# Attention scores of two heads in the two row halves of TensorE, and a first tile cut by batch

## Chip, cores and metric

One core of a Trainium2 chip. The metric is the device time of one execution in microseconds (us), lower is better.

## What is computed

A sliding-window attention (window 128, linear bias by head), then a mixture of four experts, then one dense layer with a squared ReLU, all in float32:

```python
# q, k, v: 2 batches, 8 heads, 576 positions, 64 per head
scores = q @ k.transpose(0, 1, 3, 2) / sqrt(64)
mask = (rel >= 0) & (rel < 128)                 # rel = query - key position
scores = where(mask, scores - slope[head] * abs(rel), -1e9)
attn = exp(scores - max(scores)); attn = attn / (sum(attn) + 1e-9)
x = (attn @ v), heads side by side              # 1152 tokens x 512
p = probs / (sum(probs) + 1e-9)
x = sum over e of p[:, e] * (relu(x @ w1[e]) @ w2[e])     # 4 experts, 512 -> 1024 -> 512
out = relu(x @ w_in) ** 2 @ w_out                          # 512 -> 2048 -> 512
```

## The kernel before

**Precision.** Matrices that need float32 results are split: `hi` is the value rounded to fp32r, `lo` the rest, and a product is hi·hi + lo·hi + hi·lo in fp32r, three passes of TensorE. Some early products go in plain fp32 instead, so that nothing has to be split first; each such matmul stands as two records in the profile.

**Stages.** The program has one long first stage, in which attention, the first expert's first product (g1, `hps`) and its second product (g2, `yacc`) for the first three chunks of tokens are interleaved, and then the remaining chunk, experts 1 to 3 and the dense layer. The first stage's order is made by a planner, class `Plan` (line 38): every piece of work is a task with engines that could run it and a modelled time on each, tasks it depends on, buffers it takes and a due time. `run` picks, again and again, the engine that can start first and of its tasks the most urgent one, and records that task's instructions. Each engine then executes its instructions in that order. What follows the first stage is written by another scheduler and is not touched by the change.

**Attention units.** `units` (line 627) lists the work: 4 units for query tile 0 (128 positions), each with two heads of both batches (four score matrices), then 8 units for tiles 1 and 2 and 8 for tiles 3 and 4, each two heads of one batch. Tile 4 has 64 positions and is called twin. For one unit and tile, `job_tasks` (line 833) makes the chain: scores on TensorE (`sc`, line 856), join of the two key tiles (`copy_predicated`, DVE), bias and row minimum (L917, DVE), exp (L926, ACT), inverse of the sum (DVE), scaling (POOL, ACT or DVE), transposes on TensorE (`tp`, L966), copy out (`pt`), mask halves (POOL). `pv` (line 757) then multiplies with v, two heads side by side in the two column halves of the array (`xps`: L764 in tile 0, L778 later).

**Scores.** For tiles 1 to 4, q comes twice from memory, in partitions 0 to 63 and again in 64 to 127, and k is split so that its hi part is in partitions 0 to 63 and its lo part in 64 to 127 of one tile (`khl`). So one matmul over all 128 rows gives qh·kh + qh·kl, a second one ql·kh + ql·kl: two matmuls a head, four a pair of heads (L879; twins L863). Tile 0 is not split: plain fp32 of 64 rows, always in the array's first 64 rows (L871):

```python
for g in range(G):
    if raw:
        nc.tensor.matmul(out=sc[0:n, g, :], lhsT=first_in["q", c // 2][0:D, ...],
                         rhs=first_in["k", c // 2][0:D, ...], start=True, stop=True)
        continue
    for ql in (b_["qh"].tile, b_["ql"].tile):
        nc.tensor.matmul(out=sc[0:n, g, :], lhsT=ql[:, qs], rhs=b_["khl"].tile[:, g, j0:j0 + w], ...)
```

**First tokens.** q, k and v of tile 0 are loaded by `first_load` and `first_v` (lines 1656 and 1667), then the first weights. As soon as tile 0's attention output (`xfirst`) is there, g1 starts with plain fp32 for the first four column blocks (L1839, both batches in one matmul of 256 columns), and its g2 is L1790. Later g1 is L1051 and g2 is L1287. Until there is real work, and in gaps that the planner foresees, `keep_busy` (line 554) fills TensorE with small bfloat16 matmuls on a zero tile (L560).

Of the kernel before, what the change touches and what calls it, by code (L numbers as in the profile page):

```python
# [16 lines left out]
P = 128  # L17
# [12 lines left out]
class Buf:  # L30
# [3 lines left out]
    def __init__(self, kind):  # L34
        self.kind, self.users, self.end, self.tile = kind, 0, 0.0, None


class Plan:
# [7 lines left out]
    COLD = 3.0  # L46
    WARM = 24.0
    HELD = 0.65
    SLOWED = 0.3

    def __init__(self, slots):
        self.tasks = []
        self.slots = slots
        self.held = {k: [] for k in slots}
        self.at = dict(PE=0.0, ACT=0.0, DVE=0.0, POOL=0.0, SP=0.0)
        self.port = dict(POOL=None, DVE=None)

    def add(
        self, name, opts, fn, deps=(), takes=(), bufs=(), due=0.0, follow=(), cold=True,
        shared=False  # L60
    ):
        t = dict(
            name=name, opts=opts, fn=fn, deps=[d for d in deps if d], takes=list(takes),
            bufs=list(takes) + list(bufs), due=due, end=None, follow=[d for d in follow if d],
            cold=cold, shared=shared,
        )
        for b in t["bufs"]:
            b.users += 1
        self.tasks.append(t)
        return t  # L70

    def ready(self, t):
        r = 0.0
        for d in t["deps"]:
            if d["end"] is None:
                return None
            r = max(r, d["end"] + 0.08)
        for d in t["follow"]:
            if d["end"] is None:
                return None  # L80
            r = max(r, d["start"])
        want = {}
        for b in t["takes"]:
# [3 lines left out]
            if i >= 0:  # L87
                if held[i].users:
# [4 lines left out]
    def run(self, until=None):  # L93
        todo = self.tasks
        while todo and not (until and until()):
            cand = []
            for t in todo:
# [4 lines left out]
                for eng, occ, lat in t["opts"]:  # L102
                    start = max(self.at[eng], r)
# [4 lines left out]
                cand.append((best, t))  # L108
            assert cand, [t["name"] for t in todo[:20]]
            first, _ = min(cand, key=lambda c: c[0][1])  # L110
            eng, start = first[0], first[1]
            (eng, start, occ, lat), t = min(
                (c for c in cand if c[0][0] == eng and c[0][1] <= start + self.LOOK),
                key=lambda c: c[1]["due"],
            )
            other = self.port["POOL" if eng == "DVE" else "DVE"]
            if other and (eng == "POOL" or eng == "DVE" and t["shared"]):
# [3 lines left out]
                else:  # L121
# [4 lines left out]
                    self.at["POOL"] = max(self.at["POOL"], other["start"] + other["occ"])  # L126
                occ, lat = occ + more, lat + more
            t["start"], t["end"], t["occ"] = start, start + lat, occ
            self.gap = start - self.at[eng] if start < self.WARM else 0.0
            self.at[eng] = start + occ  # L130
            if eng == "POOL" or eng == "DVE" and t["shared"]:
                self.port[eng] = t
            for b in t["takes"]:
                self.held[b.kind].append(b)
            t["fn"](eng)
            for b in t["bufs"]:
                b.users -= 1
                b.end = max(b.end, t["end"])
            todo.remove(t)
# [3 lines left out]
def kernel(  # L143
# [346 lines left out]
    def last_runs(nt):  # L490
# [17 lines left out]
        rq=3, rk=2, rv=4, qh=2, ql=2, khl=2, sc=2, tp=2, ts=5, st=5, pt=4, work=2, y=2, h=4  # L508
# [6 lines left out]
        sc=[actx.enter_context(tc.tile_pool(name="psc", bufs=2, space=PSUM))],  # L515
# [111 lines left out]
    units = [dict(bs=(0, 1), t0=0, t1=1, c=c, col=0) for c in range(NP)]  # L627
# [8 lines left out]
    task = {}  # L636

# [5 lines left out]
    def unit_tasks(u, due):  # L643
        d = units[u]
        bs, t0, t1, c = d["bs"], d["t0"], d["t1"], d["c"]
        nb = len(bs)
        G = 2 * nb
# [3 lines left out]
        full, left = divmod(nk, P)  # L651


        raw = t0 == 0
# [7 lines left out]
        def load_q(eng):  # L662
            t = b_["rq"].tile = a_tile("rq", [P, G * nq], F32)
            blocks = [(q0, q1)] if not left else [(q0, q1 - left), (q1 - left, q1)]
            for s0, s1 in blocks:
                nc.sync.dma_start(
                    out=t[:, G * (s0 - q0):G * (s1 - q0)].rearrange("p (a s) -> p a s", a=G),
                    in_=qT[bs[0], 2 * c:2 * c + 2, :, s0:s1].rearrange("a p s -> p a s"),
                )

        def load_k(eng):
            t = b_["rk"].tile = a_tile("rk", [D, G, nk], F32)
            nc.sync.dma_start(
                out=t, in_=kT[bs[0], 2 * c:2 * c + 2, :, k0:q1].rearrange("a p s -> p a s")
# [19 lines left out]
        def qh(eng):  # L694
            b_["qh"].tile = a_tile("qh", [P, G * nq], F32R)
            rounded(eng, b_["qh"].tile, b_["rq"].tile)

        def ql(eng):
            b_["ql"].tile = a_tile("ql", [P, G * nq], F32R)
            rest(eng, b_["ql"].tile, b_["rq"].tile, b_["qh"].tile)  # L700


        def kh(eng):
            b_["khl"].tile = a_tile("khl", [P, G, nk], F32R)
            rounded(eng, b_["khl"].tile[0:D], b_["rk"].tile)

        def kl(eng):
            t = b_["khl"].tile
            rest(eng, t[D:P], b_["rk"].tile, t[0:D])
# [4 lines left out]
        if raw:  # L714
            lq, lk, lv = task["first", "q", c // 2], task["first", "k", c // 2], task["first", "v"]
        else:
            lq = add("lq", dma(2 * kbytes * nq, 1 + bool(left)), load_q, takes=[b_["rq"]], due=first - 12.0,
# [5 lines left out]
        if not raw:  # L723
            tqh = add("qh", [act(G * nq), dve(G * nq)], qh, shared=True, deps=[lq], takes=[b_["qh"]],
                      bufs=[b_["rq"]], due=first - 9.0)
            tkh = add("kh", [act(G * nk), dve(G * nk)], kh, shared=True, deps=[lk], takes=[b_["khl"]],
                      bufs=[b_["rk"]], due=first - 9.1)
            tql = add("ql", [gps(G * nq), dve(G * nq)], ql, shared=True, deps=[tqh], takes=[b_["ql"]],
                      bufs=[b_["rq"], b_["qh"]], due=first - 8.2)
            tkl = add("kl", [dve(G * nk), gps(G * nk)], kl, shared=True, deps=[tkh],  # L730
# [7 lines left out]
        for i, t in enumerate(range(t0, t1)):  # L738
            split += job_tasks(
                u, i, t, add, b_, due[i], [lq, lk] if raw else [tqh, tql, tkh, tkl], G, q0, k0,  # L740
# [6 lines left out]
        if t0 == 0:  # L747
            for i in range(nb):
                mm.append((i, P, 0, 2 * i, i * P, P))
# [7 lines left out]
        def pv(eng):  # L757

            if raw:
                xps = b_["work"].tile = ps_tile("work", [P, nb * nq], "xps")  # L760
                keep_busy(xps[:, 0:P])
                for i in range(nb):
                    for a in range(2):
                        nc.tensor.matmul(  # L764
                            out=xps[a * D:(a + 1) * D, i * P:(i + 1) * P],
                            lhsT=first_in["v"][:, i, (2 * c + a) * D:(2 * c + a + 1) * D],
                            rhs=b_["pt"].tile[:, 2 * i + a, :], start=True, stop=True,
                            skip_group_check=True,
                        )
                if c == NP - 1:  # L770
# [16 lines left out]
        def evx(eng):  # L787
            if not first_x:
                first_x.append(w_tile([P, KT, CHUNKS0[0][1]], F32, "xfirst"))
            rounded(eng, first_x[0][0][:, c, :], b_["work"].tile)  # L790

        def xh_later(eng):
            rounded(eng, xh[:, c, cols], first_x[0][0][:, c, :])

        def xl_later(eng):
            rest(eng, xl[:, c, cols], first_x[0][0][:, c, :], xh[:, c, cols])
# [20 lines left out]
        tpv = add("pv", [pe(0.84 if raw else us)], pv, deps=split + [lv],  # L817
                  takes=[b_["work"]], bufs=used,
                  due=end - 1.3, follow=[prev["pv"]])
        if raw:  # L820
            add("evx", [act(nb * nq), dve(nb * nq)], evx, deps=[tpv], bufs=[b_["work"]],
                due=end - 0.9)
            teh = add("evh", [act(nb * nq), dve(nb * nq)], xh_later, shared=True,
# [1206 lines left out]
```

## Time and profile before

| | us |
|---|---|
| median of 3 runs | 641.75 (640.82 to 641.79) |
| the profiled execution, its own time | 641.43 |
| span of its instructions | 639.7 |
| TensorE busy | 633.3 (99%) |
| VectorE (DVE) busy | 470.3 (74%) |
| GpSimd (POOL) busy | 384.3 (60%) |
| ScalarE (ACT) busy | 299.3 (47%) |

The trace is one execution; times in it run from the span's first instruction. A matmul record's duration includes its latency and overlaps its neighbours, so what a matmul costs TensorE in a dense stretch is the step from its start to the next one's start, not its duration. The profile writes the used part of the array as rows times columns: 128\*128 is the whole array, 64\*128 a row half, 128\*64 a column half. PE is TensorE, PEld its weight loads.

### The profile page before, as it was taken

How to read it: one execution, taken by the hardware profiler on the slowest of the kernel's cores; microseconds unless marked ns; L12 is line 12 of the kernel's file. 1: busy time of each engine (PE TensorE's matmuls, PEld its weight loads, DVE VectorE, ACT ScalarE, POOL GpSimd, SP SyncE). 2: the span in 40 equal slices, each digit the busy share in tenths (PEclk: the TensorE clock that was granted, in tenths of full speed). 3: DMA queues.
4: the chain of work that ended last, by engine and by line, in shares of the span. 5: the costliest groups of instructions: out<-in, count | busy, mean ns of one | idle time of the engine just before them, and what ended most of it. 6: DMA issues, size and time to landing. Idle time of an engine off the chain costs nothing.

```text
span 639.7 us, 11060 instructions
## 1 busy us (share of the span) xinstructions
PE 633.3 (99%) x3929; PEld 569.2 (89%) x3929; DVE 470.3 (74%) x1023; ACT 299.3 (47%) x763; POOL 384.3 (60%) x497
## 2 busy tenths in 40 slices
PE   9999999999999999999999999999999999999997
PEld 8778899899898898998998998999999898998996
DVE  6999975378897877777777777768768767667463
ACT  6998765135354344344334334345554544343230
POOL 2589776179667447447447446346687786766531
PEclk9999999999999999999999999999999999999999
DMA  9964330222133444434434434312123223001012
GB/s 233 265 159 104 98 94 26 99 66 99 34 116 115 133 132 127 134 119 141 129 112 157 130 107 127 119 69 67 34 77 124 82 83 116 17 1 51 1 66 83
DMA packets 46983, 64.70 MB, mean 101 GB/s; under 512 B 6480, under 2 KB 29264, under 8 KB 46928
## 3 DMA queue, kind: packets, MB, share of 16 engines
q1 hardware_dynamic: 35520, 39.48, 20.9%
q10 hardware_dynamic: 11408, 24.51, 12.9%
q8 instruction: 31, 0.51, 0.3%
q14 instruction: 24, 0.20, 0.1%
HBM read 53.23 MB, written 10.75 MB: 100 GB/s over the span
## 4 chain that ended last, share of the span: by engine, by line
PE 98%; ACT 1%; DVE 0%; POOL 0%; issue 0%; POOLq 0%
PE yacc L1261 38%; PE hps L1170 35%; PE hps L1051 7%; PE yacc L1287 7%; PE xps L778 2%; PE sc L879 2%; PE tp L966 1%; PE hps L1839 1%; PE yacc L1790 1%; PE sc L560 1%; PE xtp L1353 1%; PE sc L863 1%; ACT ts L926 1%; PE sc L871 0%; PE xps L764 0%; PE ylast L1261 0%
## 5 line engine op out<-in xcount | busy, mean ns | idle before, releaser
L1261 PE MATMUL yacc<-wh,hmem 128*128 128x512 f32 x716 | 228.0, 390 | 0.0
L1261 PEld LDWEIGHTS yacc<-wh,hmem 128*128 128x128 f32 x716 | 134.6, 188 | 27.0
L1261 PE MATMUL yacc<-wl,hmem 128*128 128x512 f32 x358 | 139.9, 391 | 0.0
L536 POOL TENSOR_TENSOR wl<-wraw,wh 128x256 fp32r<-128x256 f32 (+1 forms) x79 | 74.0, 962 | 39.3 <-ACT wh L469 27.7
L536 POOL TENSOR_TENSOR hmem<-c,hmem 128x320 fp32r<-128x320 f32 (+1 forms) x64 | 59.3, 944 | 60.4 <-ACT hmem L1201 60.4
L536 POOL TENSOR_TENSOR ls<-wsum,hs 128x256 fp32r<-128x256 f32 x77 | 61.4, 825 | 54.3 <-ACT hs L414 53.6
L1185 DVE TENSOR_TENSOR u<-hps,p 128x256 f32<-128x256 f32 (+1 forms) x80 | 36.4, 455 | 65.0 <-PE hps L1170 63.1
L1181 ACT ACTIVATE p<-hps 128x256 f32<-128x256 f32 (+1 forms) x80 | 32.8, 410 | 108.8 <-PE hps L1170 108.7
L1261 PEld LDWEIGHTS yacc<-wl,hmem 128*128 128x128 f32 x358 | 67.3, 188 | 12.4
L307 DVE SCALAR_TENSOR_TENSOR wconv<-wraw,wconv 128x512 int32<-128x512 int32 x64 | 58.1, 907 | 1.3
L536 POOL TENSOR_TENSOR la<-wraw,ha 128x256 fp32r<-128x256 f32 x54 | 48.6, 919 | 16.7 <-ACT ha L400 16.7
L1205 ACT ACTIVATE hmem<-c 128x256 fp32r<-128x256 f32 (+1 forms) x72 | 31.3, 445 | 52.8 <-DVE c L1185 51.1
L1206 DVE SCALAR_TENSOR_TENSOR hmem<-c,hmem 128x256 fp32r<-128x256 f32 (+1 forms) x72 | 42.7, 614 | 14.0 <-ACT hmem L1205 13.0
L1201 ACT ACTIVATE hmem<-c 128x320 fp32r<-128x320 f32 (+1 forms) x64 | 27.3, 445 | 52.4 <-DVE c L1195 33.6
L1170 PE MATMUL hps<-ht,ls 128*128 128x320 f32 (+1 forms) x160 | 47.5, 297 | 1.3 <-POOL ls L536 1.3
L1170 PE MATMUL hps<-xh,hs 128*128 128x320 f32 (+1 forms) x160 | 47.7, 298 | 0.0
L1170 PE MATMUL hps<-ht,hs 128*128 128x320 f32 (+1 forms) x160 | 47.6, 297 | 0.0
L1170 PE MATMUL hps<-lt,hs 128*128 128x320 f32 (+1 forms) x160 | 47.4, 296 | 0.0
L1170 PE MATMUL hps<-xl,hs 128*128 128x320 f32 (+1 forms) x160 | 47.4, 296 | 0.0
L1170 PE MATMUL hps<-xh,la 128*128 128x320 f32 (+1 forms) x160 | 47.4, 296 | 0.0
L1170 PE MATMUL hps<-xl,ha 128*128 128x320 f32 (+1 forms) x160 | 47.4, 296 | 0.0
L1170 PE MATMUL hps<-xh,ls 128*128 128x320 f32 (+1 forms) x160 | 47.4, 296 | 0.0
(164 smaller groups left out, 1640.1 us busy)
## 6 DMA issues: line engine op xcount, KB each, us to landing
wraw<-in_w_dram SPq DMA_DIRECT2D x32, 512.0 KB, 3.9
wraw<-in_w_out_dram ACTq DMA_DIRECT2D x16, 512.0 KB, 3.9
w<-wconv ACTq DMA_DIRECT2D x32, 256.0 KB, 4.1
wraw<-w SPq DMA_DIRECT2D x16, 512.0 KB, 3.7
wraw<-in_w_in_dram ACTq DMA_DIRECT2D x14, 512.0 KB, 4.2
rq<-in_qT_dram SPq DMA_DIRECT2D x8, 256.0 KB, 7.7
out_dram<-y SPq DMA_DIRECT2D x7, 256.0 KB, 2.1
rk<-in_kT_dram SPq DMA_DIRECT2D x8, 192.0 KB, 5.6
```

What stands on the lines that cost most here:

```text
L307: nc.vector.scalar_tensor_tensor(out=ai, in0=raw[j][:, :, part], scalar=amount, in1=ai, op0=op, op1=ALU.bitwise_or,)
L536: e.tensor_tensor(out=out, in0=in0, in1=f32(in1), op=ALU.subtract)
L778: nc.tensor.matmul(out=xps[a * D:(a + 1) * D, x, o0:o0 + w], lhsT=held["rv"].tile[0:r, k, a * D:(a + 1) * D], rhs=held["pt"].tile[0:r, a, ...
L1051: nc.tensor.matmul(out=ps, lhsT=l_[:, k, cs], rhs=r_[:, k, cols], start=(k == 0 and r_ is xh and l_ is wh and not second), stop=(k == KT - ...
L1170: nc.tensor.matmul(out=ps, lhsT=a[l_][:, k, :], rhs=b[r_][:, k, :], start=start and k == 0 and l_ == r_, stop=stop and k == 1 and l_ == 1, ...
L1181: nc.scalar.activation(out=out, in_=x, func=ACTF.Copy)
L1185: nc.vector.tensor_tensor(out=out, in0=x, in1=y, op=ALU.add)
L1201: nc.scalar.activation(out=hh, in_=r, func=ACTF.Copy)
L1205: nc.scalar.activation(out=hh, in_=src, func=ACTF.Relu)
L1206: nc.vector.scalar_tensor_tensor(out=hl, in0=src, scalar=0.0, in1=f32(hh), op0=ALU.max, op1=ALU.subtract)
L1261: nc.tensor.matmul(out=y, lhsT=l_[:, ns], rhs=r_[:, fo, cols], start=(first and fo == 0 and j == 0), stop=(last and fo == FTQ - 1 and j == 2),
L1287: nc.tensor.matmul(out=y, lhsT=l_[:, ns], rhs=r_[:, fo, :], start=(first and j == 0), stop=(last and j == 2),)
```

## The change

1. **Scores.** q and k are loaded once, two heads in partitions 0 to 63 and 64 to 127. Both are split into hi and lo over all 128 partitions. Each score is three products of 64 rows (qh·kh, qh·kl, ql·kh); the two heads of a pair stand next to each other in the order, one in the array's first row half and one in its second, each into a PSUM bank of its own. Twins do the same with one unsplit fp32 product, in the two diagonal quarters of the array (64\*64). The two score banks are taken once and used in two halves.
2. **Tile 0.** Eight units of two heads of one batch in place of four of two heads of both. Loads, `pv`, `xfirst` and the first fp32 g1 are cut by batch to match (g1: 128 columns, twice as many matmuls).
3. **Planner.** The stage is laid out up to 600 times with due times jittered around modelled TensorE gaps, and the layout with the earliest modelled end of TensorE is recorded. Weight buffers become slots of the model (`wb`), and some modelled times and the length of the filler change.

```diff
-    units = [dict(bs=(0, 1), t0=0, t1=1, c=c, col=0) for c in range(NP)]
+    NR = B * NP
+    units = [dict(bs=(b,), t0=0, t1=1, c=c, col=b * P) for b in range(B) for c in range(NP)]
...
         def load_q(eng):
-            t = b_["rq"].tile = a_tile("rq", [P, G * nq], F32)
...
+            t = b_["rq"].tile = a_tile("rq", [P, nq], F32)
+            both = qT[bs[0], 2 * c:2 * c + 2, :, q0:q1].rearrange("a p s -> (a p) s")
+            nc.sync.dma_start(out=t, in_=both[D:D + P])
...
         def scores(eng):
-            sc = s["sc"].tile = ps_tile("sc", [P, G, w], "sc")
+            if "banks" not in state:
+                state["banks"], state["sc"] = ps_tile("sc", [P, 2, 2, 2 * P], "sc"), 0
+            sc = s["sc"].tile = state["banks"][:, :, state["sc"] % 2, 0:w]
+            state["sc"] += 1
             keep_busy(sc[:, 0, 0:P])
...
+            if raw:
+                q_, k_ = (first_in[x, c // 2][:, units[u]["bs"][0], c % 2, :] for x in "qk")
+                terms = [(q_, k_)]
+            elif twin:
+                terms = [(b_["rq"].tile[:, t * P - q0:], b_["rk"].tile[:, j0:j0 + w])]
+            else:
...
+                terms = [(qh, kh), (qh, kl), (ql, kh)]
+            for j, (q_, k_) in enumerate(terms):
+                for a in range(2):
+                    rows, o = slice(a * D, (a + 1) * D), a * n if twin else 0
                     nc.tensor.matmul(
-                        out=sc[0:n, g, :], lhsT=first_in["q", c // 2][0:D, g // 2, 2 * (c % 2) + g % 2, :],
...
+                        out=sc[o:o + n, a, :], lhsT=q_[rows], rhs=k_[rows], start=(j == 0),
+                        stop=(j + 1 == len(terms)), skip_group_check=True,
                     )
...
-        us = G * (0.25 if raw else 2 * max(0.107, w * 0.00047))
+        us = 0.25 if raw or twin else 3 * max(0.107, w * 0.00047)
...
-    def first_load(what, half):
+    def first_load(what, half, b):
...
+            nc.tensor.matmul(
+                out=hb["ps"][:, at], lhsT=wtask["raw", wi][:, k, cs],
+                rhs=first_x[0][0][:, k, at], start=begin, stop=(k == KT - 1),
+                skip_group_check=True,
+            )
...
-        early = plan.at["PE"] < 1.0 and plan.gap > 2.0
-        lead, each = (0.6, 0.11) if early else (-0.2, 0.08)
+        lead, each = (-0.9, 0.107) if plan.gap > 3.0 else (-0.05, 0.056)
...
+        for _ in range(self.ROUNDS):
+            if not waits:
+                break
+            to, _ = chance.choices(waits, [w for _, w in waits])[0]
+            trial = list(due)
+            for i, s in enumerate(starts):
+                if to - 10.0 < s < to + 3.0 and chance.random() < 0.15:
+                    trial[i] += chance.gauss(0.0, 4.0)
+            end, o, w = self.lay(trial)
+            if end is not None and end <= least:
+                least, order, waits, due = end, o, w, trial
+                starts = [t["start"] for t in self.tasks]
```

From the g2 group that follows the last `pv` of the first stage, every engine's order is the same in both programs. Ahead of that, three places show what moves. The names: `sc` scores, `tp` transposes, `xps` the products with v, `hps` g1, `yacc` g2, `first` tile 0's q, k and v, `xfirst` its attention output, `wraw` unsplit weights.

TensorE, tile 0 up to the first g1 products, before:

```order
L966 MATMUL tp<-ident,ts 128x128 x4
L764 MATMUL xps<-pt,first 64x128 x4
L966 MATMUL tp<-ident,ts 128x128 x4
L1839 MATMUL hps<-xfirst,wraw 128x256
L764 MATMUL xps<-pt,first 64x128 x8
L1839 MATMUL hps<-xfirst,wraw 128x256 x3
L879 MATMUL sc<-khl,qh 128x256
```

and in the change:

```order
L811 MATMUL xps<-pt,first 64x128 x2
L1898 MATMUL hps<-xfirst,wraw 128x128
L811 MATMUL xps<-pt,first 64x128 x2
L1015 MATMUL tp<-ident,ts 128x128 x2
L931 MATMUL sc<-first 128x128 x2
L1015 MATMUL tp<-ident,ts 128x128 x2
L1898 MATMUL hps<-xfirst,wraw 128x128 x2
L811 MATMUL xps<-pt,first 64x128 x2
L1015 MATMUL tp<-ident,ts 128x128 x2
L1898 MATMUL hps<-xfirst,wraw 128x128
```

The first g1 product stood behind the `pv` of two units of four heads; now it stands behind that of two units of two heads. Scores, `pv` and transposes of the other units, which lay ahead of it, now alternate with g1 in smaller pieces.

TensorE in the middle of the first stage, before (g2, a transpose, the scores of one tile of one unit, g1):

```order
L1287 MATMUL yacc<-wh,hmem 128x512
L966 MATMUL tp<-ident,ts 128x128
L879 MATMUL sc<-khl,qh 128x256
L879 MATMUL sc<-khl,ql 128x256
L879 MATMUL sc<-khl,qh 128x256
L879 MATMUL sc<-khl,ql 128x256
L1051 MATMUL hps<-xh,wh 128x256
```

and in the change, two such places, the second one a twin:

```order
L1015 MATMUL tp<-ident,ts 128x128 x2
L931 MATMUL sc<-khl,qh 128x256 x4
L931 MATMUL sc<-khl,ql 128x256 x2
L1336 MATMUL yacc<-wh,hmem 128x512
...
L1336 MATMUL yacc<-wh,hmem 128x512
L931 MATMUL sc<-rk,rq 64x192 x2
L1100 MATMUL hps<-xh,wh 128x256
```

Four matmuls over the whole array become six over row halves (three pairs), and a twin's four become two over quarters; whole-array work stands on both sides.

SyncE's queue at the start, before:

```order
L1663 DMA first<-in_qT_dram 64x4x128 x4
L1663 DMA first<-in_kT_dram 64x4x128 x2
L1671 DMA first<-in_v_dram 128x2x512
L227 DMA wraw<-in_w_dram 128x4x256
```

and in the change:

```order
L1712 DMA first<-in_qT_dram 128x2x128
L1712 DMA first<-in_kT_dram 128x2x128
L1712 DMA first<-in_qT_dram 128x2x128 x3
L1712 DMA first<-in_kT_dram 128x2x128
L1720 DMA first<-in_v_dram 128x2x512
L275 DMA wraw<-in_w_dram 128x4x256
```

Each load is as large as before, but the first one of q and the first one of k (on ACT's queue, as before) now hold all that the first two units need. The first weights keep their place behind the same bytes.

## Rows read from the trace of the kernel before

**Rows 1.** The page, part 1: busy us, share of the span and instructions.

```profile
PE 633.3 (99%) x3929; PEld 569.2 (89%) x3929; DVE 470.3 (74%) x1023; ACT 299.3 (47%) x763; POOL 384.3 (60%) x497
```

**Rows 2.** Busy time by stretch: length, PE, PEld, DVE, ACT, POOL, PEclk, DMA, GB/s.

```profile
17.28:20.00 2.72, 2.72 (x25) 2.05 (x24) 2.55 (x4) 2.61 (x9) 2.04 (x1) 1.00 0.91 186
20.00:120.00 100.00, 99.96 (x754) 85.99 (x753) 78.06 (x289) 73.62 (x239) 72.27 (x120) 1.00 0.43 111
```

**Rows 3.** Timeline of PE: the g2 group with which the common order begins.

```profile
120.09 0.40 PE L1287 MATMUL yacc<-wh,hmem 128*128 128x512 f32 x1
```

**Rows 4.** Chain that ended last, 0 to 125 us: start, us, what.

```profile
1.06 5.62 PE sc L560 x51
...
11.38 3.20 ACT ts L926 x16
...
17.44 0.43 PE hps L1839 x2
```

**Rows 5.** Timeline of PE, scores before: start, us, what.

```profile
36.38 0.28 PE L879 MATMUL sc<-khl,qh 128*128 128x256 f32 x1
36.50 0.28 PE L879 MATMUL sc<-khl,ql 128*128 128x256 f32 x1
...
103.58 0.27 PE L863 MATMUL sc<-khl,qh 128*128 128x192 f32 x1
103.69 0.27 PE L863 MATMUL sc<-khl,ql 128*128 128x192 f32 x1
```

**Rows 6.** Timeline of PE in narrow windows, where the used part of the array changes.

```profile
9.54 0.33 PE L560 MATMUL sc<-idle 128*128 128x128 bf16 x3
...
9.71 0.22 PE L560 MATMUL sc<-idle 128*128 128x128 bf16 x1
9.86 0.37 PE L871 MATMUL sc<-first 64*128 64x128 f32 x1
...
10.07 0.38 PE L871 MATMUL sc<-first 64*128 64x128 f32 x2
...
10.18 0.38 PE L871 MATMUL sc<-first 64*128 64x128 f32 x2
...
11.63 0.27 PE L871 MATMUL sc<-first 64*128 64x128 f32 x1
11.84 0.33 PE L966 MATMUL tp<-ident,ts 128*128 128x128 f32 x1
...
12.00 0.38 PE L966 MATMUL tp<-ident,ts 128*128 128x128 f32 x2
...
36.74 0.28 PE L879 MATMUL sc<-khl,ql 128*128 128x256 f32 x1
36.95 0.32 PE L778 MATMUL xps<-pt,rv 128*64 128x128 f32 x1
...
118.55 0.39 PE L1051 MATMUL hps<-xh,wh 128*128 128x256 f32 x1
118.78 0.28 PE L1051 MATMUL hps<-xl,wh 128*128 128x256 f32 x1
```

**Rows 7.** Timeline of PE, one whole pv in column halves and what follows it.

```profile
36.95 1.96 PE L778 MATMUL xps<-pt,rv 128*64 128x128 f32 x24
38.84 0.44 PE L966 MATMUL tp<-ident,ts 128*128 128x128 f32 x2
```

**Rows 8.** SyncE's timeline, then DMA issues (KB each, us from issue to landing).

```profile
0.80 3.02 SPq L1663 DMA_DIRECT2D first<-in_qT_dram  x4
...
5.83 0.47 SPq L227 DMA_DIRECT2D wraw<-in_w_dram  x1
...
first<-in_qT_dram SPq DMA_DIRECT2D x1, 128.0 KB, 3.8
...
first<-in_qT_dram SPq DMA_DIRECT2D x1, 128.0 KB, 4.7
...
wraw<-in_w_dram SPq DMA_DIRECT2D x1, 512.0 KB, 6.7
```

More of the change, by code (lines that the diff above doesn't have):

```diff
@@ L53, in __init__ @@
         self.slots = slots
-        self.held = {k: [] for k in slots}
-        self.at = dict(PE=0.0, ACT=0.0, DVE=0.0, POOL=0.0, SP=0.0)
-        self.port = dict(POOL=None, DVE=None)
+        self.gap = 0.0
     def add(
@@ L63, in add @@
             name=name, opts=opts, fn=fn, deps=[d for d in deps if d], takes=list(takes),
-            bufs=list(takes) + list(bufs), due=due, end=None, follow=[d for d in follow if d],
-            cold=cold, shared=shared,
+            bufs=list(takes) + list(bufs), due=due, follow=[d for d in follow if d],
+            cold=cold, shared=shared, next=[],
         )
@@ L68, in add @@
             b.users += 1
+        for d in t["deps"] + t["follow"]:
+            d["next"].append(t)
         self.tasks.append(t)
@@ L91, in ready, with lay @@
         return r
[L93 to L97, printed above, removed]
+    def lay(self, due):
+        self.held = {k: [] for k in self.slots}
+        at = dict(PE=0.0, ACT=0.0, DVE=0.0, POOL=0.0, SP=0.0)
+        port = dict(POOL=None, DVE=None)
+        cand, order, waits = [], [], []
+        for i, t in enumerate(self.tasks):
+            t["due_now"], t["open"] = due[i], len(t["deps"]) + len(t["follow"])
+            for b in t["bufs"]:
+                b.left, b.end = b.users, 0.0
+            if not t["open"]:
+                cand.append(t)
+        while cand:
+            ways, first = [], None
+            for t in cand:
                 r = self.ready(t)
@@ L131, in run @@
+            order.append((t, eng, gap if start < self.WARM else 0.0))
+            at[eng] = start + occ
             if eng == "POOL" or eng == "DVE" and t["shared"]:
-                self.port[eng] = t
+                port[eng] = t
             for b in t["takes"]:
                 self.held[b.kind].append(b)
+            for b in t["bufs"]:
+                b.left -= 1
+                b.end = max(b.end, t["end"])
+            cand.remove(t)
+            for d in t["next"]:
+                d["open"] -= 1
+                if not d["open"]:
+                    cand.append(d)
@@ new lines, in lay, with run @@
+        return (at["PE"] if len(order) == len(self.tasks) else None), order, waits
+    def run(self):
+        chance = random.Random(1)
+        due = [t["due"] for t in self.tasks]
+        least, order, waits = self.lay(due)
+        assert least is not None, [t["name"] for t in self.tasks if t["open"]][:20]
+        starts = [t["start"] for t in self.tasks]
[10 more added lines that the diff above has]
+                least, order, waits, due = end, o, w, trial
+                starts = [t["start"] for t in self.tasks]
+        self.least = least
+        for t, eng, gap in order:
+            self.gap = gap if eng == "PE" else 0.0
@@ L1811, in item_tasks @@
         due = T0 + T1 * ch + ITEM * f
-        us = [u for u in range(len(units)) if u // NP == ch]
+        us = [NR + (ch - 1) * NP + c for c in range(NP)]
         wi = 2 * (f // FTQ)
-        split = it < 4
-        raw = ch == 0 and f < RAW1
+        split = raw = ch == 0 and f < RAW1
         half = it % 2
@@ L1910 @@
     N1 = 3 * FT
-    parted = sorted(range(PER), key=lambda i: (FTQ * order[i][1] < (RAW1, RAW2)[order[i][2]], i))
     for i in range(PER):
```

343 lines of the change are left out of this document (171 added, 172 removed).

## The prediction

> **What bounds the kernel now.** I read the page first: TensorE is busy 633.3 of 639.7 us [rows 1], so the question is which of its time is work. From the end of the first stage on (the g2 group at 120.09 [rows 3]) both programs have the same order on every engine, so only what lies before it can differ, and the end of the kernel moves with that instant. The table by stretch then splits the first stage [rows 2]: from 17.28, where the first g1 product starts, to 120 TensorE has no free time, while DVE, ACT and POOL have 78, 74 and 72 of 100 us. The table of waits agrees: for that stretch it has no row for TensorE, which waited for nobody. Before 17.28 it is another matter. The chain of waits [rows 4] goes through filler until 6.68 (tile 0's q and k are not there), then through ACT's sixteen exps, 3.2 us of them on the chain, and reaches g1 at about 17.3. So the first stage is a head of 17.3 us that waits for loads and a chain over engines, and 102.8 us (17.28 to 120.09) of TensorE back to back. A gain must shorten the head or take TensorE time out of the dense part; relief for the other engines is worth nothing there.
>
> **The dense part: products.** Costs are steps from start to start.
> - Scores of tiles 1 to 3: a whole-array matmul of 256 columns takes 0.12 us [rows 5], four a job, 0.48. After: three pairs. If the two heads of a pair run side by side, a pair is 0.12 and a job 0.36. 24 jobs: -2.9 us.
> - That pairs run side by side is shown for column halves only: one `pv` of 24 records starts at 36.95 and is followed at 38.84, 1.89 us [rows 7]. Its 16 records of 128 columns at 0.11 (the step inside L871, 10.07 to 10.18 [rows 6]) and 8 of 256 at twice that would take 3.5 one after the other. I take row halves to do the same; both ends are kept below.
> - Twins: 4 x 0.11 [rows 5] become two fp32 matmuls of 192 columns side by side, two records each at 1.5 x 0.11, 0.33. 8 jobs: -0.9.
> - Tile 0's g1: 64 records of 128 columns instead of 32 of twice the width, 0.11 against 0.22: nothing.
> - Work that was in the head and now lies behind the first g1, because g1 comes sooner in the order: ten transposes, two `pv` pairs and one score pair (two records a head), 16 steps of 0.11. +1.8.
> Together -2.0 us.
>
> **The dense part: changes of the array's form.** This is the term that decides. Where TensorE goes from the whole array to a part of it, the next matmul starts late, and so does the one after it [rows 6]. Going in: filler steps are 0.055 (three from 9.54 to 9.71), but the first L871 starts 0.15 after the last filler; the last whole-array score at 36.74 is followed at 36.95, 0.21 where 0.12 is the step. That is 0.09 late twice. The second matmul then follows the first after 0.21 (9.86 to 10.07) where the step is 0.11: the first one's weights were not loaded ahead, 0.10 more. Going out: 11.63 to 11.84 is 0.21 for 0.11, 0.09 to 0.10 late again, and the first step after it is 0.16 for 0.11 with transposes and 0.23 for 0.12 with g1 (118.55 to 118.78), 0.05 to 0.11 more. So a change costs 0.14 to 0.20; I take 0.18.
> Counted in the order from the first g1 to the common part, the program before changes form 18 times (nine stretches of `pv`). The change does it 85 times: `pv` now has 13 stretches, and nearly every score job stands alone between whole-array work (22 stretches in row halves, 8 twins in quarters, two of the former next to a `pv`). 67 x 0.18 = +12.1 us.
> Bounds: if the weights could load while the array empties, 0.09 a change, +6.0; with all of the worst steps 0.20, +13.4; if the row half cost no change at all, 0.
>
> **The head.** The first two units need one load of q and one of k. Before, a unit needs two of each: the first q load is issued at 0.80 and lands 3.8 later, at 4.6; the second lands 4.7 after its issue near 1.6, at 6.3 [rows 8]. So scores start 1.7 us sooner. The first g1 cannot start before its weights: issued at 5.83, landed 6.7 later, at 12.5 [rows 8], and the same bytes stand ahead of them in the change. In between, the first unit needs two exps instead of four before its transposes. I put g1 at 12.6 and add 0.5 us for waits on ACT and POOL while the other units come in: 13.1 in place of 17.28, -4.2. Bounds: 12.6 (-4.7), and 15.6 if the chain behind the scores takes as long as now (-1.7).
>
> **What costs nothing.** Each split of q and k is over half as many columns, each unit loads half the q; tile 0 has four more rounds of small instructions on DVE and ACT. All of it is on engines that TensorE does not wait for after 17.3, with 20 us and more free in 100 [rows 2]. Were that cover gone, tile 0's four more rounds of some four small instructions at 0.2 us (3.20 for 16 on ACT [rows 4]) would cost 3.2. Waits of scores for their PSUM halves stay as they are: two jobs in flight, as with two tiles.
>
> **Sum.** -2.0 + 12.1 - 4.2 = +5.9 us on the profiled execution's 641.4 (span 639.7 and 1.7 around it; 0.3 below the median of the runs): **647.3**. With the bounds of the change of form alone 641.2 to 648.6 (635.2 at zero), and a late head adds up to 2.5: 651.1.
>
> **A rule weighed.** All sixteen matmuls of one L871 stretch use the same row half and follow each other in 0.11 [rows 6], a step that holds no extra weight load. The Trainium skill, TensorE: Matmul & The Clock Gate, Part 3 (what overlaps and what doesn't), says that a weight load overlaps running matmuls only if it goes to another row group. By that rule the second and third pair of a job would each wait 0.10 for their weights: 24 x 2 x 0.10 = 4.8 more, 652.1. The rows here speak against it.
>
> **Rivals.**
> 1. *A change of form into row halves is cheap* (faster). The saving decides as soon as a change costs less than (4.2 + 2.0) / 67 = 0.09 us. At zero the time is 641.4 - 6.2 = 635.2, in general 635 to 640. For it: there is one clean entry into a row half in the trace (9.86), behind filler, and none out of or into fp32r work. Against it: that entry and its exit (11.84) are as late as those of the column halves. 0.18.
> 2. *Balance*: weights load under the emptying array, 0.09 a change; 641.4, within 1.3 us. For it, only that fp32r is another type; against it, the 0.10 of 9.86 to 10.07 and of 118.55. 0.06.
> 3. *Pairs do not run side by side*: the change does not do what it says. Each job is 0.72 instead of 0.36 (+8.6), a twin 0.66 (+2.6): 658.5; with weights waited for in every pair, 652.1 as above. For it: no row has two row halves in use. Against: the column halves. 0.08.
> 4. *The head is not shortened*: g1 at 15.6 or later, because ACT still has sixteen exps and now more small copies between them; 650 to 653. For it: ACT is on the chain with 3.2 us [rows 4] and has 2.61 of 2.72 us at 17.28 [rows 2]. Against: g1 needs only the first units. 0.08.
>
> **Chances and range.** The forecast with 0.14 to 0.20 a change and g1 between 12.6 and 15 has 0.60: 644 to 651. It is the likeliest, so 647.3 is the prediction. The range 640.5 to 652.5 takes in that, the balance, most of the late head and the edges of rivals 1 and 3; it leaves out a fifth. About 0.2% (1.3 us) is what a measurement of this kernel can tell from no change. Faster is rival 1 and the lower edge of 2, 0.19; the same 0.05; slower the rest, 0.76.
>
> **What would show it.** Right: in the timeline of the changed kernel the score pairs start within 0.01 us of each other and step by 0.12, but the first pair of a job starts some 0.2 after its whole-array neighbour and the second pair another 0.2 later; the first g1 is near 13; the common g2 group starts near 126 instead of 120.09; TensorE still waits for nobody between. Wrong: score jobs whose neighbours follow in 0.12 (rival 1), halves that start 0.12 apart (rival 3), a first g1 beyond 15 or a wait row of TensorE over 2 us (rival 4).

## The result, and the profile after

| | before | after |
|---|---|---|
| median, same chip | 641.70 us (640.82 to 641.79) | 648.21 us (647.82 to 649.95) |
| ratio | | 1.011, 95% interval 1.0089 to 1.013 |
| profiled execution, its own time and span | 641.43, 639.7 | 648.43, 646.7 |
| first g1 starts | 17.28 | 14.67 |
| common g2 group starts | 120.09 | 127.03 |
| dense part between them | 102.8 | 112.4 |

The change makes the kernel 1.1% slower; the forecast was 647.3 us, with a range of 640.5 to 652.5. The group with which the common order begins starts 6.9 us later, the span is 7.0 us longer: all of the difference lies in the first stage. The page of after, part 1, answers to [rows 1]: TensorE has 5.3 us more to do, the other three engines have 6 to 10 us less.

```profile
PE 638.6 (99%) x3994; PEld 563.9 (87%) x3994; DVE 463.1 (72%) x1039; ACT 293.5 (45%) x770; POOL 374.1 (58%) x506
```

Busy time by stretch of after, for [rows 2]; the first row is the dense part:

```profile
14.67:127.03 112.36, 112.34 (x880) 87.88 (x879) 77.45 (x316) 73.33 (x265) 63.79 (x125) 1.00 0.31 89
20.00:120.00 100.00, 99.98 (x779) 77.85 (x780) 72.25 (x296) 67.22 (x241) 61.27 (x119) 1.00 0.34 98
```

TensorE has no free time there. Its table of waits for 0 to 130 us (line, who is waited for: us in total, times, longest) has three rows, all from the head:

```profile
PE sc L607 <- DVE st L966: 1.8, 2, 1.2
PE sc L607 <- DVE idle L1684: 1.1, 1, 1.1
PE sc L931 <- DVE st L966: 0.5, 1, 0.5
```

So it is TensorE's own steps that grew. Its timeline, two score jobs of tiles 1 to 4 between a g1 and a transpose:

```profile
46.51 0.28 PE L1100 MATMUL hps<-xl,wh 128*128 128x256 f32 x1
46.63 0.28 PE L1100 MATMUL hps<-xh,wl 128*128 128x256 f32 x1
46.84 0.50 PE L931 MATMUL sc<-khl,qh 64*128 64x256 f32 x4
47.18 0.28 PE L931 MATMUL sc<-khl,ql 64*128 64x256 f32 x2
47.30 0.40 PE L931 MATMUL sc<-khl,qh 64*128 64x256 f32 x4
47.54 0.28 PE L931 MATMUL sc<-khl,ql 64*128 64x256 f32 x2
47.75 0.33 PE L1015 MATMUL tp<-ident,ts 128*128 128x128 f32 x1
```

Three pairs of the second job take 47.30 to 47.54 for two and 0.21 for the last: two products side by side in 0.12, as forecast. The price stands at the edges: the g1 step before the stretch is 0.21 instead of 0.12, the first job's first two pairs take 0.34 instead of 0.24, the last pair 0.21.

Added up over the whole dense part, each step compared with the usual step of the same product (0.12 for 256 columns of g1, 0.11 for a transpose, 0.12 for a pair of scores, and so on), the difference between the two traces comes out as an estimate in three terms:

| of the dense part, us | before | after |
|---|---|---|
| products at their usual steps | 98.4 | 96.4 |
| lateness of the steps at changes of form | 2.9 (18 changes) | 15.5 (86 changes) |
| all other lateness | 1.5 | 0.5 |

So the products fall by 2.0 us, the changes cost 12.5 us more, 0.18 for each of them in after, and 1.0 us of other lateness goes.

### The profile page after: what moved, and what is told of

It reads as the page before. It is cut to its first block, busy times and chain, and to the rows that moved or that the text cites. A ratio compares the mean times of both kernels' runs of the same rounds, so it can differ in the third digit from the quotient of the medians.

```text
span 646.7 us, 11217 instructions
## 1 busy us (share of the span) xinstructions
PE 638.6 (99%) x3994; PEld 563.9 (87%) x3994; DVE 463.1 (72%) x1039; ACT 293.5 (45%) x770; POOL 374.1 (58%) x506
## 4 chain that ended last, share of the span: by engine, by line
PE 98%; DVE 1%; ACT 0%; POOL 0%; issue 0%; DVEq 0%
PE yacc L1310 38%; PE hps L1219 35%; PE hps L1100 7%; PE yacc L1336 7%; PE sc L931 3%; PE xps L824 2%; PE tp L1015 2%; PE hps L1898 1%; PE yacc L1856 1%; PE sc L607 1%; PE xtp L1402 1%; PE xps L811 0%; DVE ts L966 0%; PE ylast L1310 0%; POOL ls L584 0%
## 5 line engine op out<-in xcount | busy, mean ns | idle before, releaser
L584 POOL TENSOR_TENSOR wl<-wraw,wh 128x256 fp32r<-128x256 f32 (+1 forms) x81 | 76.7, 973 | 40.8 <-ACT wh L517 28.8
L1310 PEld LDWEIGHTS yacc<-wl,hmem 128*128 128x128 f32 x358 | 67.3, 188 | 12.5
```

The source lines that it names most:

```text
L584: e.tensor_tensor(out=out, in0=in0, in1=f32(in1), op=ALU.subtract)
L1310: nc.tensor.matmul(out=y, lhsT=l_[:, ns], rhs=r_[:, fo, cols], start=(first and fo == 0 and j == 0), stop=(last and fo == FTQ - 1 and j == 2),
```

## Experiments

The theory: a change of the array's form costs some 0.18 us, and there are 68 more of them (86 against 18 in the two traces; the forecast counted 85); the first tile by batch gives back less than that. The rivals: the row-half products themselves, the first tile's eight units, the planner's new order. "After" is the changed kernel; the dense part is from the first g1 to the common g2 group. "No waits" means TensorE busy for 99.9 of 100 us or more between 20 and 120 us.

### Twice as many changes of form, and a control

```diff
                 terms = [(qh, kh), (qh, kl), (ql, kh)]
+                if True:
+                    for a in range(2):
+                        rows = slice(a * D, (a + 1) * D)
+                        nc.tensor.matmul(
+                            out=sc[0:n, a, :], lhsT=terms[0][0][rows], rhs=terms[0][1][rows],
+                            start=True, stop=True, skip_group_check=True,
+                        )
+                    nc.tensor.matmul(
+                        out=sc[:, 0, 0:P], lhsT=idle, rhs=idle, start=True, stop=True,
+                        skip_group_check=True,
+                    )
```

The control has the two added blocks in the other order.

> Ahead of each of the 24 full score jobs of tiles 1 to 4, one pair of extra row-half products and then one extra whole-array product of the idle tile, all of them written over by the job's own first products. Counted in the order: 48 more changes of array form than after. My theory: 48 x 0.18 = 8.6 us for the changes and 24 x (0.12 + 0.056) = 4.2 us for the extra products, so the stretch from the first g1 to the common g2 is about 125.3 us and the time about 661 us; against the control with the same extra products in the other order (7 more changes) 41 x 0.18 = 7.4 us longer. Rival, a change costs little of itself and the time sits in the row-half products: both kernels the same within 1 us, near 652.5 us.

> The same extra products as in the doubled kernel, but the whole-array one first and the row-half pair behind it, next to the job's own row-half products: 7 more changes of array form than after (where two stretches touched before). My theory: 4.2 us for the extra products and 7 x 0.18 = 1.3 us, about 653.7 us. Rival, the row-half products themselves are dear: 24 pairs at 0.3 us or more, 656 us or more, and no less than the doubled kernel.

One execution each: 659.93 us, and 653.84 for the control. The dense parts are 123.6 and 117.5 us, both without waits: 11.2 and 5.1 more than after. Equal products in another order differ by 6.1 us for 41 changes, 0.15 each; against after, 11.2 less 4.2 for the extra products is 7.0 for 48, again 0.15. The rival (row-half products are dear, both kernels alike) falls. The timeline of the doubled kernel shows where the price sits:

```profile
41.64 0.39 PE L931 MATMUL sc<-khl,qh 64*128 64x256 f32 x2
41.96 0.23 PE L935 MATMUL sc<-idle 128*128 128x128 bf16 x1
42.12 0.50 PE L942 MATMUL sc<-khl,qh 64*128 64x256 f32 x4
```

The extra pair takes 0.32 (0.12, 0.10 as the first after an entry, 0.10 at the exit), the whole-array filler after it 0.16 instead of 0.056. This added stretch in row halves costs 0.3 us more than its products, 0.15 a change. It is less than the 0.18 of after because the filler stands alone between two changes: its one late step is the last of the one and the first of the other, where elsewhere two steps are late.

### The heads one after the other

```diff
-            for j, (q_, k_) in enumerate(terms):
-                for a in range(2):
+            for a in range(2):
+                for j, (q_, k_) in enumerate(terms):
```

> In the score jobs the three products of the first head, then the three of the second, in place of pair by pair; as many products and as many changes of array form as after. My theory, the two products of a pair run side by side: at most one pair still can, so a job of six products takes 5 to 6 steps of 0.12 us in place of 3, 24 x (0.24 to 0.36) = 5.8 to 8.6 us, and the time is 654 to 657 us. Rival, the two halves take turns anyway and the rows' starts 3 to 5 ns apart mislead: 648 us, within 1 us.

655.19 us, one execution: the number that my theory expected, but for another reason, so it came out by luck. The common g2 group starts 6.7 us later than in after, but the first g1 already 4.9 us later (19.57), though the programs are the same up to there (a job of the first tile has one product a head). From the first g2 of plain fp32 to the same group the two kernels take as long: 37.24 to 133.71 here, 30.51 to 127.03 in after, 96.5 us each. In the head, TensorE's steps are doubled; the timeline of this kernel and then its stretch of 8 to 10 us:

```profile
7.28 1.87 PE L607 MATMUL sc<-idle 128*128 128x128 bf16 x16 [1.16 <-DVE st L966]
...
8.00:10.00 2.00, 2.00 (x19) 1.80 (x17) 0.00 (x0) 0.29 (x2) 0.72 (x2) 1.00 0.91 300
```

After's same sixteen fillers take 1.05 us (below). So the program order of the products costs nothing, and here is why, in the same kernel's timeline:

```profile
45.14 0.51 PE L931 MATMUL sc<-khl,qh 64*128 64x256 f32 x4
45.48 0.28 PE L931 MATMUL sc<-khl,ql 64*128 64x256 f32 x2
45.60 0.40 PE L931 MATMUL sc<-khl,qh 64*128 64x256 f32 x4
45.84 0.28 PE L931 MATMUL sc<-khl,ql 64*128 64x256 f32 x2
```

In the program a job is qh, qh, ql of one head and then qh, qh, ql of the other. They start as four qh and two ql, in pairs 2 to 12 ns apart here, 0.12 from pair to pair once the stretch has begun: the second head's products run beside the first's. That both halves work at once is confirmed more strongly than by the forecast's own test; my expectation that order would matter was wrong.

### Whole-array scores, first tile by batch

Tiles 1 to 4 get back the loads, splits, scores and join of before (L662 to L731 and L856 to L899 there); units of the first tile, PSUM halves and planner stay as after.

```diff
-                terms = [(qh, kh), (qh, kl), (ql, kh)]
...
+                for g in range(G):
...
+                    for x in ("qh", "ql"):
+                        nc.tensor.matmul(
+                            out=sc[:, g, :], lhsT=b_[x].tile[:, qs],
+                            rhs=b_["khl"].tile[:, g, j0:j0 + w], start=(x == "qh"),
+                            stop=(x == "ql"), skip_group_check=True,
+                        )
```

> Tiles 1 to 4 score as before the change (whole-array products of stacked high and low parts), the first tile by batch and the planner's search stay as after the change. My theory (about 0.18 us for each change of array form): from the first g1 to the common g2 there are 30 changes where after has 86, so 56 x 0.18 = 10.1 us go, and 3.8 us of products come back; that stretch falls from 112.4 to about 106.1 us, the first g1 stays near 14.7 us, the time is about 642 us (640.5 to 643.5), 6 us under after. Rival, the eight units of the first tile or the new order cost the time, not the row halves: it stays at 647 us or more.

646.12 us, ratio to before 1.0072 (1.0055 to 1.0089): between the two theories. The first g1 is at 14.45, the dense part 110.15, 2.2 us shorter than after where the count gave 6.3. The stretch shows what came instead:

```profile
20.00:120.00 100.00, 98.90 (x745) 83.49 (x744) 79.09 (x292) 73.50 (x234) 75.52 (x126) 1.00 0.43 111
```

TensorE is idle for 1.1 of 100 us, and a record's duration includes its latency, so that short waits hide behind it: in its timeline thirteen steps, scattered from 20 to 108 us, are 0.15 to 0.4 us longer than the same step elsewhere, 3.3 us in all. That is nearly the 3.6 us by which the measurement exceeds the count (106.5, with the 0.17 a change that after showed). Whole-array scores bring DVE, ACT and POOL back to 79, 74 and 76 of 100. That TensorE waits for these engines in the long steps is the likely reading, but the table of waits has only two rows for it, both for DVE, 0.5 us together. Before had as much to do there, and only three steps of this kind, 0.5 us in all.

### The splits done twice

```diff
-            rounded(eng, b_["qh"].tile, b_["rq"].tile[:, 0:nqs])
+            for _ in range(2):
+                rounded(eng, b_["qh"].tile, b_["rq"].tile[:, 0:nqs])
```

The same for `ql`, `kh` and `kl`.

> After the change with each rounding and each remainder of q and k of tiles 1 to 4 done twice into the same place, so that ScalarE, VectorE and GpSimd have about as much of this work as with whole-array scores; TensorE's order is untouched. Theory A (the prediction's step that the relief of the other engines is worth nothing, since TensorE waits for none of them): 648.2 us, within 1 us. Theory B (in the order by batch the relief is what keeps TensorE from waiting; without it come the waits of 3.6 us that the whole-array kernel with 30 changes showed): 650 to 652 us, with TensorE busy by about 1 us of 100 less.

656.94 us, 1.0237 (1.0223 to 1.0251): 8.7 us over after, more than theory B. TensorE's order is that of after, the dense part 120.5 us. The row of the dense part and the longest rows of the waits from 14 to 137 us:

```profile
20.00:120.00 100.00, 96.54 (x719) 73.94 (x718) 77.86 (x292) 75.35 (x259) 68.18 (x122) 0.98 0.34 99
```

```profile
PE hps L1104 <- DVE xl L584: 1.0, 1, 1.0
PE sc L935 <- DVE st L963: 0.8, 1, 0.8
PE tp L1019 <- ACT ts L1002: 0.6, 1, 0.6
PE sc L935 <- DVE st L970: 0.6, 1, 0.6
PE sc L935 <- DVE ql L584: 0.6, 1, 0.6
```

Three engines with 22 to 32 us of 100 to spare hold TensorE up, so a share of free time is no measure of cover. Not all of the 8.7 us is waiting: after the longest waits, from 64 to 68 us, the granted clock is 0.57 to 0.58 and twelve g1 steps take 0.21 instead of 0.12, so 1.1 us there are slower steps. After's order is planned for the shorter splits. In that order the change's relief is therefore not worth nothing; it keeps the dense part free of waits. Whether an order planned for the longer splits would need it was not tried.

### Is it the eight units or the searched order?

Before, with after's class `Plan` and filler rule and nothing else; and after without the planner's trials:

```diff
-    ROUNDS = 600
+    ROUNDS = 0
```

> The kernel before with nothing of the change but the planner (its constants, its 600 trials and its filler rule): the first tile by two batches, whole-array scores everywhere, 19 changes of array form between the first g1 and the common g2 by the order (18 in before), 0.9 us of products moved behind the first g1. Theory A, the waits of 3.6 us that whole-array scores showed with the first tile by batch come from the first tile's eight units: without them that stretch is 103.4 us as counted, TensorE busy for at least 99.9 of 100 us, the first g1 at 16.3 to 17.3 us, and the time 641 to 642 us. Theory B, they come from the searched order, which leaves no slack: that stretch is 105 us or more and the time 643.5 us or more.

> After the change with no trials of the planner (its first order stands): 87 changes of array form between the first g1 and the common g2 in place of 86, the same products and units. The planner's own figures differ by 1.5 us. Theory A, the search brings about what it reckons: that stretch is 113 to 114.5 us and the time 649 to 650.5 us. Theory B, the search takes away slack and costs time: 647.5 us or less.

Before with the new planner: 646.53 us, 1.0073 (1.006 to 1.0086), dense part 105.9, TensorE idle for 1.7 of 100 us. That is theory B's number, and it speaks against the eight units as the only cause, since this kernel has the four of before. But its first g1 is late as well (19.35): TensorE ran at 1.2 GHz there.

```profile
8.00:16.00 8.00, 8.00 (x46) 6.88 (x46) 4.66 (x32) 4.39 (x23) 0.00 (x0) 0.50 1.09 296
20.00:40.00 20.00, 18.76 (x105) 13.36 (x104) 16.98 (x57) 16.63 (x54) 12.47 (x17) 1.00 0.83 227
```

Most of the waiting follows that late head, so the order alone is not isolated. After without trials: 649.61 us (649.21 to 650.07), dense part 113.8, TensorE busy 99.30 of 100: theory A. With row-half scores the search is worth some 1.4 us of the dense part; the times of the two kernels overlap. So the searched order is not what makes after slower than before.

### More slack in the plan

Whole-array scores as above, without the later fillers of the next experiment, with the plan changed:

```diff
-            r = max(r, d["end"] + 0.08)
+            r = max(r, d["end"] + (0.2 if t["opts"][0][0] == "PE" else 0.08))
```

> The kernel with whole-array scores for tiles 1 to 4 and the first tile by batch (29 changes of array form between the first g1 and the common g2), planned with 0.2 us of slack ahead of each TensorE task in place of 0.08 us and with 3,000 trials in place of 600, and without the fillers ahead of the first tile's later scores. The same kernel with 0.08 us of slack took 110.15 us for that stretch where 29 or 30 changes and the products give 106.5 us; the rest looks like short waits of TensorE for other engines. Theory A, these waits come from the order: with slack that stretch is 106.7 to 108 us, and with a first g1 between 12.6 and 14.7 us the time is 641 to 644 us. Theory B, VectorE and GpSimd, busier by 6.8 and 14 us of 100 with whole-array scores, cannot keep up in any order: that stretch stays at 110 us and the time at 644 to 646 us.

649.34 us, 1.0123 (1.0108 to 1.0138): neither. The granted clock was 0.50 from 8 to 18 us, so beyond the first g1 (14.52), and the dense part grew to 113.5 with TensorE busy 97.02 of 100. Theory A falls for this order; as the head was slowed too, B is not shown by it.

### The head without its later fillers

```diff
-            keep_busy(sc[:, 0, 0:P])
+            if not raw or state["sc"] == 1:
+                keep_busy(sc[:, 0, 0:P])
```

The experiment asks why the first g1 of after came at 14.67 and not at the forecast's 13.1. After's timeline of TensorE ahead of it:

```profile
6.92 1.05 PE L607 MATMUL sc<-idle 128*128 128x128 bf16 x16 [1.16 <-DVE st L966]
7.90 0.71 PE L931 MATMUL sc<-first 64*128 64x128 f32 x8
9.23 1.05 PE L607 MATMUL sc<-idle 128*128 128x128 bf16 x16 [0.61 <-DVE st L966]
10.21 0.49 PE L931 MATMUL sc<-first 64*128 64x128 f32 x4
10.64 0.40 PE L607 MATMUL tp<-idle 128*128 128x128 bf16 x4
10.87 0.39 PE L1015 MATMUL tp<-ident,ts 128*128 128x128 f32 x2
11.74 0.49 PE L931 MATMUL sc<-first 64*128 64x128 f32 x4 [0.48 <-DVE st L966]
```

The fillers write into the PSUM half that DVE still reads. They wait for it like the scores, run only then, and the scores come behind them, twice 0.98 us.

> After the change without the filler products ahead of the first tile's scores, all but the first burst (34 products fewer on TensorE ahead of the first g1; nothing else moves). My theory: in after two bursts of 16 fillers of 1.05 us each run behind the wait for the PSUM half that VectorE reads, and so stand on the way to the first g1; without them the first g1 starts up to 2.1 us earlier, at 12.6 us in place of 14.7, and the time is about 646.2 us. Rival, the head is set by VectorE's chain of scores, maxima and sums, and the fillers only fill: 648 us, within 0.6 us. Second rival, the fillers hold the granted clock at full speed: without them it falls to half in the head and the time is 648.5 us or more.

647.17 us, 1.0085 (1.0068 to 1.0102): about 1 us under after, with runs of 646.52 to 647.97 that overlap after's. The first g1 starts at 14.06, 0.6 earlier and not 2.1. A line of this kernel's timeline, and its rows for 8 to 14 us:

```profile
9.67 1.23 PE L932 MATMUL sc<-first 64*128 64x128 f32 x8
...
8.00:10.00 2.00, 1.94 (x12) 1.31 (x14) 1.34 (x11) 1.47 (x9) 0.79 (x3) 0.50 0.91 301
10.00:12.00 2.00, 2.00 (x16) 1.60 (x14) 1.83 (x13) 1.05 (x5) 0.72 (x2) 0.50 1.05 374
12.00:14.00 2.00, 2.00 (x13) 1.02 (x11) 0.71 (x5) 0.84 (x3) 0.00 (x0) 0.50 1.08 365
```

Both readings of the fillers hold: they stand on the path, and without them the granted clock is 0.50 (1.2 GHz) from 8 to 14 us, where after has 1.00. The scores that start at 11.74 in after start at 9.67 here: the 2.1 us are there. From these scores to the first g1 it then takes 4.4 us instead of 2.9, at the lower clock, and that eats most of the gain. The first rival does not fall with it: between the scores TensorE still waits for DVE's row minima in both kernels.

### Fewer changes by grouping

Both tiles of a unit score in one stretch, as one task that takes both PSUM halves; then the same with the planner told of 0.18 us for a change of form (8,000 trials).

```diff
+        def both(eng):
+            scores(eng)
+            d["then"](eng)
...
+                    if eng == "PE" and self.form(t) != form:
+                        occ, lat = occ + 0.18, lat + 0.18
```

> After the change with the scores of both tiles of a unit in one stretch (tiles 1 and 2, or 3 and 4, one behind the other; both halves of the PSUM tile taken at once): from the first g1 to the common g2 there are 64 changes of array form in place of 86, with as many products. My theory: 22 x 0.18 = 4.0 us fewer, and 0.4 us of products that move ahead of the first g1, so that stretch is about 108.0 us and the time about 644 us. Rival, both halves are then full together, and TensorE waits for VectorE to empty them in each of 16 units: what the changes give back goes into waits, 646.5 us or more, with waits in the chain that after does not have.

> Row-half scores with both tiles of a unit in one stretch, and the planner told of 0.18 us for each change of array form: 51 changes between the first g1 and the common g2 in place of 64. My theory: 13 x 0.18 = 2.3 us under the grouped kernel's 108.25 us, so about 106.0 us, a first g1 at 14.7 to 15.3 us, and a time of 642 to 643 us, level with before. Rival, the new order makes TensorE wait: 644.6 us or more.

Grouped: 644.63 us, 1.0046 (1.0031 to 1.0061), 3.6 under after; dense part 15.35 to 123.60, 108.25 for 108.0 expected. Less the 0.4 us of products that moved, 3.7 us for 22 changes, 0.17 each. The rival (waits for the halves) falls: TensorE is busy 99.53 of 100, and its only row of waits there is 0.5 us for ACT's `hfirst`. With the price in the plan: 643.35 us, 1.0032 (1.0021 to 1.0043). The span falls by 1.1 us, but not where the theory has it. The first g1 starts 1.4 us earlier (13.94). From there to the first g1 products of the last chunk (384 columns) the two kernels take as long, 109.6 us each: the steps at changes give back about 2.0 us, and new waits take it, among them the first and the last of these rows (the second is in the grouped kernel too):

```profile
PE tp L1029 <- DVE ts L1005: 0.8, 1, 0.8
PE hps L1923 <- ACT hfirst L1856: 0.5, 1, 0.5
PE hps L1125 <- DVE hmem L1964: 0.3, 1, 0.3
```

The same price in the plan of the whole-array kernel:

> Whole-array scores for tiles 1 to 4, the first tile by batch, and the planner told of 0.18 us for each change of array form (8,000 trials, aimed at waits and at changes): 16 changes between the first g1 and the common g2 in place of 30, with the same products. My theory: that stretch is 103.9 us (106.5 by the count for the kernel with 30 changes, less 14 x 0.18 = 2.5 us) plus what TensorE waits for other engines, between nothing and the 3.6 us of the kernel with 30 changes; the first g1 at 14.5 us; the time 639.8 to 643.4 us, so under before's 641.7 us if the waits are under 1.9 us. Rival, changes are not what the time goes to in whole-array kernels: 646 us, as with 30 changes.

646.17 us, 1.0072 (1.0059 to 1.0085), as without it, though the first g1 starts 1.0 us earlier (13.42). The changes did fall to 16, but TensorE is busy only 97.09 of 100: waits took what the changes gave. No version tried beats before; the priced grouping, 0.3% behind it, is the nearest.

## Why the forecast held, step by step

- **Where the time lies.** Right: nothing differs after the common group but its start.
- **Changes of form**, +12.1 us for 67 at 0.18: right in kind and size. From the lengths alone, with the forecast's own -2.0 us of products, after's dense part gives (9.6 + 2.0) / 68 = 0.17; grouping gives 0.17, doubling 0.15. Step by step it is 0.18 a change and +12.5 us. The term decides the result, and undoing a third of the changes gave back 3.6 of the 6.5 us.
- **Products**, -2.0: right, 98.4 to 96.4 us at their usual steps. Pairs step by 0.12, so rival 3 falls, and so does the 0.10 of waiting for weights in the second and third pair: the pairs of 47.30 to 47.54 don't wait. The rule weighed in the forecast, of the Trainium skill, TensorE: Matmul & The Clock Gate, Part 3 (what overlaps and what doesn't), that a weight load overlaps running matmuls only in another row group, does not fit these rows.
- **Rivals 1 and 2** (a change at 0.09 or less): fallen, by every price above. **Rival 4**, g1 at 15.6 or later: did not come; 14.67 lies between it and the forecast.
- **The head**, -4.2: mis-sized. It gave -2.6. I had the weights (12.5) and 0.5 for small waits set the first g1. The weights landed at 11.1; what set it is the wait of the scores for the PSUM halves that DVE still reads, with 2.1 us of filler behind that wait and the scores behind the filler. "Waits of scores for their PSUM halves stay as they are" is the sentence that failed: the head has eight units to pass through two halves, where it had four.
- **The dense part** as a whole, 102.8 - 2.0 + 12.1 = 112.9: 112.4. The forecast took all of before's 102.8 us for work and changes; 1.0 us of it was other lateness that after does not have. That part of the agreement is luck, and it hides some of the head's miss: the head's 1.6 us late and this 0.5 early put the profiled execution 1.1 above 647.3.
- **Relief of the other engines, nothing**: right for the sum, since in the dense part before's TensorE waited for none of them and after's waits for none. Wrong as a statement of cover: "20 us and more free in 100" hid nothing when the splits were doubled.

What stays open: why whole-array scores wait in each of the three orders that the new planner made for them with the first tile by batch, and in the fourth with before's units, when before's own order has next to none. The first tile by batch in an order like before's was not tried.

## What to carry to other kernels

Before packing two small products into halves of the array, count the stretches, not the products: each costs 0.3 to 0.4 us for its two edges, so a job that saves 0.12 has to share its stretch with others to pay. Count them in the order that is really issued, and give a planner their price, with its other estimates in step. And an engine's free share is no cover by itself: doubling the splits on engines that were idle for a quarter of the time or more cost 8.7 us.

## What the runs showed of the hardware

- Products in different row halves start in another order than the program has them: qh, qh, ql of one head and then of the other ran as pairs, 96.5 us for the stretch in both orders. In the program as compiled from that kernel the weight loads and products of all 24 jobs still stand in the order of the source, three of one row half and then three of the other, so the pairs are formed behind the compiler. The Trainium skill has, in TensorEngine Tiling (Array Packing), Key Properties, tiles (parts of the array) that load weights and multiply in parallel; the pairs agree with that. The Trainium skill, TensorE: Matmul & The Clock Gate, Part 3 (what overlaps and what doesn't), says that matmuls start and end strictly in program order; the starts of this case's rows differ from that, and the rows decide.
- The granted clock of a stretch can read 1.00 while steps are doubled: sixteen fillers took 1.87 us against 1.05, both under rows of 1.00. In this case the steps of known products are the surer sign.
- Thirty-four fillers fewer in the head, and the granted clock was 0.50 from 8 to 14 us where it had been 1.00; TensorE had been busy 1.23 of the 3 us from 5 to 8, with them 1.84. In before with the new planner it was 0.50 too, from 8 to 16 us, and there TensorE had been busy 1.76 of the same 3 us.
